# K and V of a batch multiplied a chunk ahead, in front of the next chunk's queries, in a three-stage kernel on one core

## The chip, the cores and the metric

One Trainium2 chip, one of its cores. The metric is the device time of the whole program in microseconds (us), the median over the timed runs. A profiled execution is a run of its own, with its own time beside its span.

## The reference

Three stages in a row. Linear attention (8 batches, 8 heads, 576 tokens, 64 wide), a layer of three maxima and an output product, then routed experts (top 2 of 8):

```python
kv  = einsum('bhsd,bhse->bhde', k, v)            # 64x64 for each batch and head
out = einsum('bhsd,bhde->bhse', q, kv)
x   = out / sqrt(mean(out * out, -1) + 1e-6) * g_norm     # then as (4608, 512)
h   = maximum(maximum(x @ w1, x @ w2), x @ w3)            # 512 -> 768
x   = h @ w_out                                           # 768 -> 512
# top-2 of 8 experts by noisy logits; out[token] += weight * (relu(x @ w1[e]) @ w2[e])
```

## The kernel before

The 4608 tokens go through attention and the first layer in nine chunks (0 to 8) of 512 tokens. A batch has 576 tokens, so chunk c reads the products of K and V (here: K/V) of batches c - 1 and c; they lie in two tiles `kvt`, one for even and one for odd batches.

A chunk c from 1 on has 18 steps g. Each step first runs `misc1(c, g)` and then one first product `g1` (12 matmuls; 512 columns wide, in chunk 1 only 256), which takes the next of a ring of four PSUM banks (`hbank`). VectorE or ScalarE reads the bank afterwards. After the 18 steps comes the window, `window(c)`: the second products `g2` (L399), into the other four banks (`abank`), mixed with the preparation of the next chunk's input. Chunk 0 is the start and is ordered by a planner with costs; the two K/V blocks of batches 0 and 1 are multiplied in it.

`misc1` holds what is put between the steps. At step 0 SP is given the noise, the next chunk's queries (`load_q`, L169) and, in three parts, K and V of the next batch (`load_kv`: a megabyte into `KV0` at L152, a megabyte into a staging tile `STG[b % 2]` at L156, a quarter megabyte into `STG[2]` at L160). At step 7 (chunk 1) or 10 (later) the routing of the chunk before is computed, with two small bf16 products on TensorE (L457, L458) and four scatters on POOL (L472). At step 10 of chunks 1 to 6 the K/V of batch c + 1 is multiplied, `kv_all` (L187) into four banks of the second ring, a bank for two heads, and copied to `kvt` by four copies (L198). At steps 12 to 15 `attend(c + 1, ...)` makes the next chunk's attention: step 12 multiplies the queries (`ao`, L213, four banks of the second ring), squares on ScalarE (L230) and reductions on VectorE (L234) follow, then the normed rows are split in planes (into `KV0`) and turned by DMA transposes on SP (L301). At step 12 (chunk 1) or 14 (later) a copy on VectorE (L480) overwrites a column of the rows that the first scatters read, and four more scatters follow.

A K/V block is 40 matmuls of the program: 32 over 128 rows of K (a tile of 128x64 of the array, two of them side by side), and 8 over the last 64 rows (tiles of 64x64). The trace has two records for each. The queries' block is 64 matmuls of 64x64 tiles. The first and second products use the whole array, 128x128. Every engine works through its instructions in the order of the program; SP gives out its transfers in order too, and one whose buffer is not free yet holds up those behind it.

```python
        for g in range(18):          # chunk c
            misc1(c, g)
            if c > 0:
                g1(c, g)
```

Of the kernel before, what the change touches and what calls it, by code (L numbers as in the profile page):

```python
# [18 lines left out]
NB, NH, S, D = 8, 8, 576, 64  # L19
# [63 lines left out]
def body(tc, A, dbg=None):  # L83
    nc = tc.nc
    PE, ACT, DVE, POOL, SP = nc.tensor, nc.scalar, nc.vector, nc.gpsimd, nc.sync
# [19 lines left out]
    KB = [sb1.tile([128, 256], F, name=f"kvt{i}") for i in range(2)]  # L105
# [15 lines left out]
    def hbank():  # L121
        cnt["h"] += 1
        return HB[(cnt["h"] - 1) % 4]

    def abank():
        cnt["a"] += 1
        return AC[(cnt["a"] - 1) % 4]
# [19 lines left out]
    def quarters(t):  # L147
        return [t[:, i * 512:(i + 1) * 512] for i in range(4)]

    def load_kv(b, part):  # L150
        if part == 0:
            SP.dma_start(KV0, A["kv4"][b, 0])  # L152
            kvraw[b] = [quarters(KV0)]
        elif part == 1:
            t = STG[b % 2]
            SP.dma_start(t, A["kv4"][b, 1])  # L156
            kvraw[b].append(quarters(t))
        else:
            t = STG[2]
            SP.dma_start(t[:, 0:512], A["kvr"][b])  # L160
            kvraw[b].append(t[:, 0:512])
# [3 lines left out]
    def qv(c):  # L165
        return qbuf[c][:, 0:2048].rearrange("p (a t) -> p a t", a=4)
# [8 lines left out]

    HALF = [slice(0, 64), slice(64, 128)]

    def kv_mm(b, p, s, out):
        r = kvraw[b]
        for h in range(2):  # L180
            if s < 4:
                k, v = r[s // 2][2 * (s % 2):2 * (s % 2) + 2]
                o = p * 128 + h * 64
            else:
                k, v = r[2][HALF[p // 2], 0:256], r[2][HALF[p // 2], 256:512]
                o = p % 2 * 128 + h * 64
            PE.matmul(out[HALF[h], :], k[:, o:o + 64], v[:, o:o + 64], start=s == 0, stop=s == 4)  # L187

    def kv_all(b, banks):
        for p in range(4):  # L190
            for s in range(4):
                kv_mm(b, p, s, banks[p][:, 0:64])
        for p in (0, 2, 1, 3):
            kv_mm(b, p, 4, banks[p][:, 0:64])

    def kv_outs(b, banks):
        for p in range(4):
            (ACT.copy if p % 2 else DVE.tensor_copy)(KB[b % 2][:, p * 64:(p + 1) * 64], banks[p][:, 0:64])  # L198
# [3 lines left out]
    def ao(c, j, banks):  # L202
        for h in range(2):
            ao_bank[c, 2 * j + h] = banks[h]
        for i in range(2):
            t0 = (2 * j + i) * 128
            for p in range(4):
                o = slice(i * 256 + p * 64, i * 256 + (p + 1) * 64)
                for x in range(2):
                    t = t0 + x * 64  # L210
                    kb = KB[(c * CT + t) // S % 2]
                    for h in range(2):
                        PE.matmul(banks[h][HALF[x], o], qv(c)[HALF[h], p, t:t + 64],  # L213
                                  kb[HALF[h], p * 64:(p + 1) * 64], start=True, stop=True)
# [6 lines left out]
    def norm_a(c, i, x=None):  # L221
        if x is None:
            x = XNS[xn_n[0] % 4]
            xn_n[0] += 1
        norm_sq(c, i, x)
        norm_red(c, i)
# [9 lines left out]
    def norm_b1(c, i0, i1):  # L236
        s = [ST[:, r, i0:i1, :] for r in range(2)]
        DVE.tensor_scalar(s[0], s[0], 1.0 / 64, 1e-6, op0=OP.mult, op1=OP.add)
        ACT.activation(s[1], s[0], AF.Ln)
        ACT.activation(s[1], s[1], AF.Exp, scale=-0.5)  # L240

    def norm_b2(c, i0, i1):
        s = [ST[:, r, i0:i1, :] for r in range(4)]
        DVE.tensor_tensor(s[2], s[1], s[1], op=OP.mult)
        DVE.scalar_tensor_tensor(s[2], s[2], -0.5, s[0], op0=OP.mult, op1=OP.mult)
        DVE.scalar_tensor_tensor(s[3], s[2], 1.5, s[1], op0=OP.add, op1=OP.mult)

    def norm_c(c, i):
        x = xn_of[c, i]
        DVE.tensor_tensor(x.rearrange("p (h e) -> p h e", h=8),  # L250
                          ao_bank[c, i].rearrange("p (h e) -> p h e", h=8),
                          ST[:, 3, i, :].unsqueeze(2).to_broadcast([128, 8, 64]), op=OP.mult)
# [51 lines left out]
    def planes_in(c, b):  # L304
# [8 lines left out]
        ACT.activation(hi, m, AF.Copy, scale=gn[:, 0:1])  # L313
        DVE.scalar_tensor_tensor(lo, m, gn[:, 0:1], hi.bitcast(F), op0=OP.mult, op1=OP.subtract)

    def attend(c, n):
        if n == 0:
            for j in range(2):
                ao(c, j, [abank(), abank()])
        if n < 2:  # L320
            for b in (2 * n, 2 * n + 1):
                norm_a(c, b)
        if n == 1:
            norm_b1(c, 0, 4)
            norm_b2(c, 0, 4)
        if n in (2, 3):
            j = n - 2
            for b in (2 * j, 2 * j + 1):
                norm_c(c, b)
                planes_out(c, b)  # L330
            planes_turn(c, j)
# [589 lines left out]
    def misc1(c, g):  # L921
        if c == 1 and g == 0:
            fills()
        if c == 1 and (g == 0 or 8 < g < 14):
            f = max(g - 8, 0)
            hsplit(f, early(f), 0, 256)
        if g == 0:
            SP.dma_start(noise[c % 2], A["noise"][c])
        if g == 0 and 0 < c < NCH - 1:
            load_q(c + 1)  # L930
            if c + 1 < NB:
                for i in range(3):
                    load_kv(c + 1, i)
        if c > 0:
            if g == 1:
                ra[c] = route_a(c - 1)
            if 0 < g < 5:
                next(ra[c], None)
            if g == (7 if c == 1 else 10):
                route_b(c - 1)  # L940
                scatter(c - 1, 0)
                if c > 1:
                    zero_out(c - 2)
            if g == (12 if c == 1 else 14):
                scatter(c - 1, 1)
        if 0 < c < NB - 1 and g == 10:
            banks = [abank() for p in range(4)]
            kv_all(c + 1, banks)
            kv_outs(c + 1, banks)
        if 0 < c < NCH - 1 and g >= 12:  # L950
            attend(c + 1, g - 12)
        if c == NCH - 1:
            if g == 11:
                spec_pick()
                load_regs(0, spi[0:1, 0:1], spi[0:1, 1:2])
                regE[1] = regE[0]
                regS[1] = SP.value_load(spi[0:1, 2:3], min_val=0, max_val=DUMMY)
                for p in range(2):
                    load_pair(p)
            if g == 12:  # L960
                load_rows(0)
            if g > 14:
                splits(1)
# [41 lines left out]
    c = NCH - 1  # L1005
# [11 lines left out]
    n, g, q, r2, r1, a = (s8[:, k] for k in (0, 1, 2, 3, 4, 10))  # L1017
# [432 lines left out]
```

## Time and profile before

| | us |
|---|---|
| median of 3 runs | 1510.59 |
| lowest and highest | 1510.12, 1511.88 |
| the profiled execution's own time | 1503.61 |
| its span in the trace | 1501.8 |
| granted TensorE clock in it | 0.998 |

How to read it: the span runs from the first to the last profiled instruction; the profiled execution's own time also has what lies around it. Times in the rows are counted from the start of the span. PE is TensorE's matmuls, PEld its weight loads, DVE VectorE, ACT ScalarE, POOL GpSimd, SP the engine that gives out most transfers. Matmuls overlap, so what a block takes is read from start to start, not from the durations.

### The profile page before, as it was taken

How to read it: one execution, taken by the hardware profiler on the slowest of the kernel's cores; microseconds unless marked ns; L12 is line 12 of the kernel's file. 1: busy time of each engine (PE TensorE's matmuls, PEld its weight loads, DVE VectorE, ACT ScalarE, POOL GpSimd, SP SyncE). 2: the span in 40 equal slices, each digit the busy share in tenths (PEclk: the TensorE clock that was granted, in tenths of full speed). 3: DMA queues.
4: the chain of work that ended last, by engine and by line, in shares of the span. 5: the costliest groups of instructions: out<-in, count | busy, mean ns of one | idle time of the engine just before them, and what ended most of it. 6: DMA issues, size and time to landing. Idle time of an engine off the chain costs nothing.

```text
span 1501.8 us, 22899 instructions
## 1 busy us (share of the span) xinstructions
PE 1476.2 (98%) x9190; PEld 1260.4 (84%) x9190; DVE 749.5 (50%) x1513; ACT 644.2 (43%) x1020; POOL 223.3 (15%) x332
## 2 busy tenths in 40 slices
PE   6999999999999999999999999999999999999997
PEld 6889989898989888888888878887888888888886
DVE  6985545454444444458344454553454374444443
ACT  4653524242424233334444454544454364444443
POOL 0000111102020202023211102202211111110112
PEclk9999999999999999999999999999999999999999
DMA  7412435142332303083776668767565587554555
GB/s 315 144 70 99 152 117 149 72 149 86 126 114 99 121 29 122 0 240 107 200 200 140 173 217 227 194 186 199 135 162 137 147 216 196 132 135 140 139 121 108
DMA packets 160724, 218.43 MB, mean 145 GB/s; under 512 B 124320, under 2 KB 124704, under 8 KB 145120
## 3 DMA queue, kind: packets, MB, share of 16 engines
q1 hardware_dynamic: 140624, 165.14, 35.0%
q0 software_dynamic: 19984, 51.73, 15.1%
q8 instruction: 74, 1.21, 0.3%
q14 instruction: 42, 0.34, 0.1%
HBM read 137.86 MB, written 51.72 MB: 126 GB/s over the span
## 4 chain that ended last, share of the span: by engine, by line
PE 54%; POOL 0%; issue 0%; ACT 0%; POOLq 0%
PE bank L1242 26%; PE bank L1180 26%; PE bank L1194 1%; PE bank L1283 1%; PE bank L1298 0%; PE bank L399 0%; POOL out L1216 0%; PE bank L1205 0%; ACT W L334 0%; PE bank L1289 0%; ACT xn L1247 0%; POOLq L1398 0%; ACT RA L406 0%; PE bank L1136 0%; POOL spacer L1215 0%
## 5 line engine op out<-in xcount | busy, mean ns | idle before, releaser
L353 PE MATMUL bank<-B,W 128*128 128x512 f32 (+1 forms) x2184 | 453.1, 367 | 2.2 <-ACT W L532 2.1
L353 PEld LDWEIGHTS bank<-B,W 128*128 128x128 f32 x2184 | 376.4, 188 | 70.4 <-ACT W L532 2.5
L1242 PE MATMUL bank<-W,B 128*128 128x512 f32 x1704 | 411.2, 390 | 0.0
L1242 PEld LDWEIGHTS bank<-W,B 128*128 128x128 f32 x1704 | 318.6, 188 | 64.5
L1180 PE MATMUL bank<-B,W 128*128 128x512 f32 (+4 forms) x1536 | 361.0, 374 | 0.0
L1180 PEld LDWEIGHTS bank<-B,W 128*128 128x128 f32 x1536 | 278.1, 188 | 53.7 <-issue 4.4
L335 DVE TENSOR_TENSOR W<-G,W 128x1024 fp32r<-128x1024 f32 x168 | 203.0, 1224 | 121.8 <-ACT W L334 121.3
L1184 ACT ACTIVATE B<-bank 128x512 fp32r<-128x512 f32 (+4 forms) x152 | 85.8, 565 | 334.3 <-PE bank L1180 334.3
L1185 DVE SCALAR_TENSOR_TENSOR B<-bank,B 128x512 fp32r<-128x512 f32 (+4 forms) x152 | 98.7, 649 | 249.0 <-ACT B L1184 248.4
L334 ACT ACTIVATE W<-G 128x1024 fp32r<-128x1024 f32 x168 | 175.4, 1055 | 43.5 <-PE bank L1242 24.9
L399 PE MATMUL bank<-W,B 128*128 128x256 f32 (+1 forms) x1296 | 161.0, 284 | 0.4 <-DVE B L361 0.2
L399 PEld LDWEIGHTS bank<-W,B 128*128 128x128 f32 x1296 | 159.5, 188 | 1.6 <-ACT RA L406 0.5
L472 POOL DMA_INDIRECT Xg<-RA,si x72 | 70.7, 981 | 582.0 <-issue 403.7
L371 DVE TENSOR_TENSOR hm<-hm,bank 128x512 f32<-128x512 f32 (+1 forms) x107 | 69.6, 651 | 115.2 <-PE bank L353 109.8
L1216 POOL DMA_INDIRECT out<-xn,idt x36 | 59.2, 1644 | 402.9 <-ACT xn L1247 397.6
L357 ACT ACTIVATE B<-hm 128x512 fp32r<-128x512 f32 (+1 forms) x53 | 32.2, 607 | 172.4 <-DVE hm L371 172.4
L1180 PE MATMUL bank<-xlo,W 128*128 128x512 f32 (+2 forms) x288 | 73.3, 376 | 0.0
L1180 PEld LDWEIGHTS bank<-xlo,W 128*128 128x128 f32 x288 | 52.5, 188 | 9.8
L369 ACT ACTIVATE hm<-bank 128x512 f32<-128x512 f32 (+1 forms) x54 | 30.4, 564 | 64.1 <-PE bank L353 52.2
L406 ACT COPY RA<-bank 128x256 uint16<-128x256 uint16 x72 | 25.6, 372 | 68.6 <-DVE RA L406 63.2
L1216 POOL DMA_INDIRECT out<-hm,idt x20 | 31.9, 1593 | 131.2 <-ACT hm L1247 127.4
L361 DVE TENSOR_TENSOR B<-hm,B 128x512 fp32r<-128x512 f32 (+1 forms) x53 | 35.1, 661 | 32.2 <-ACT B L357 32.2
(230 smaller groups left out, 1034.8 us busy)
## 6 DMA issues: line engine op xcount, KB each, us to landing
G<-mw SPq DMA_DIRECT2D x84, 1024.0 KB, 5.1
G<-w1s SPq DMA_DIRECT2D x12, 1024.0 KB, 4.9
kv<-kv SPq DMA_DIRECT2D x8, 1024.0 KB, 7.1
G<-kv SPq DMA_DIRECT2D x8, 1024.0 KB, 9.2
RB<-qT SPq DMA_DIRECT2D x8, 1024.0 KB, 4.9
G<-mw SPq DMA_DIRECT2D x16, 512.0 KB, 6.4
out<-pad POOLq DMA_DIRECT2D x5, 1280.0 KB, 6.5
out<-pad POOLq DMA_DIRECT2D x2, 1536.0 KB, 6.7
```

Source lines behind the costliest of these rows:

```text
L334: ACT.activation(w[:, 0:1024], src, AF.Copy)
L335: DVE.tensor_tensor(w[:, 1024:2048], src, w[:, 0:1024].bitcast(F), op=OP.subtract)
L353: PE.matmul(bank[:, 0:t1 - t0], w_in(g)[:, a, k, s], x[b][:, k, t0:t1], start=n == 0 and k == 0, stop=n == 2 and k == 3)
L361: DVE.tensor_tensor(h[:, 1], hm, h[:, 0].bitcast(F), op=OP.subtract)
L371: DVE.tensor_tensor(hm, hm, bank, op=OP.max)
L399: PE.matmul(x2b[i][z][:, 0:hi - lo], h[:, a, s], w[:, b, lo:hi], start=f == 0 and n == 0, stop=f == 5 and n == 2)
L472: i = POOL.indirect_dma_start(out=Xg, out_offset=bass.IndirectOffsetOnAxis(ap=idx, axis=0), in_=src, in_offset=None)
L1180: PE.matmul(bank[:, 0:n], w[:, a, k, s], x[b][:, k, 0:n], start=z == 0, stop=z == 11)
L1184: ACT.activation(h[:, 0, 0:n], bank[:, 0:n], AF.Relu)
L1185: DVE.scalar_tensor_tensor(h[:, 1, 0:n], bank[:, 0:n], 0.0, h[:, 0, 0:n].bitcast(F), op0=OP.max, op1=OP.subtract)
L1216: d = POOL.indirect_dma_start(out=A["out"], out_offset=bass.IndirectOffsetOnAxis(ap=idt[u % 3][:, i:i + 1], axis=0), in_=y, in_offset=None ...
L1242: PE.matmul(obank[i], h[:, a, s], w[:, b, ff % 2, :], start=ff == 0 and n == 0, stop=ff == 7 and n == 2)
```

## The change

K/V of a batch is multiplied one chunk earlier than before: at step 12 of chunk c the block of batch c + 2 runs, directly before the products of the queries of chunk c + 1, which use the K/V of batches c and c + 1. Batch 2 is multiplied in chunk 1 at step 5, and batch 3 is loaded right after it; after that K and V of batch c + 2 are loaded at step 0 of chunk c. The block takes two banks of the ring of the first products, two pairs of heads to a bank side by side (the `start` and `stop` marks are set once for a bank), and is copied to `kvt` by two copies, behind the queries' products in the program.

```diff
-    def kv_mm(b, p, s, out):
+    def kv_mm(b, p, s, out, two=False):
...
-            PE.matmul(out[HALF[h], :], k[:, o:o + 64], v[:, o:o + 64], start=s == 0, stop=s == 4)
+            PE.matmul(out[HALF[h], :], k[:, o:o + 64], v[:, o:o + 64], 
+                      start=s == 0 and not (two and p % 2), stop=s == 4 and not (two and p % 2 == 0))
...
+    def kv_next(b, c=None):
+        two = [hbank() for i in range(2)]
+        banks = [two[p // 2][:, p % 2 * 64:p % 2 * 64 + 64] for p in range(4)]
+        kv_all(b, banks, True)
+        if c is not None:
+            ao_all(c)
+        for i in range(2):
+            (ACT.copy if i else DVE.tensor_copy)(KB[b % 2][:, i * 128:i * 128 + 128], two[i][:, 0:128])
+
+    def ao_all(c):
+        for j in range(2):
+            ao(c, j, [abank(), abank()])
+
     def attend(c, n):
         if n == 0:
-            for j in range(2):
-                ao(c, j, [abank(), abank()])
+            if c + 1 < NB:
+                kv_next(c + 1, c)
+            else:
+                ao_all(c)
...
             load_q(c + 1)
-            if c + 1 < NB:
-                for i in range(3):
-                    load_kv(c + 1, i)
+            for i in range(3):
+                if c == 1:
+                    load_kv(2, i)
+                elif c + 2 < NB:
+                    load_kv(c + 2, i)
...
-        if 0 < c < NB - 1 and g == 10:
-            banks = [abank() for p in range(4)]
-            kv_all(c + 1, banks)
-            kv_outs(c + 1, banks)
+        if c == 1 and g == 5:
+            kv_next(2)
+            for i in range(3):
+                load_kv(3, i)
```

## Rows read from the trace of the kernel before

**Rows 1.** The page, part 1: busy time, share of the span, instructions.

```profile
PE 1476.2 (98%) x9190; PEld 1260.4 (84%) x9190; DVE 749.5 (50%) x1513; ACT 644.2 (43%) x1020; POOL 223.3 (15%) x332
```

**Rows 2.** Waits of TensorE, 34 to 720 us: us in total, times, longest.

```profile
PE bank L353 <- ACT W L532: 2.1, 1, 2.1
...
```

**Rows 3.** Windows: each engine's busy us (instructions), PEclk, DMA share, GB/s.

```profile
182.00:720.00 538.00, 537.84 (x3904) 466.20 (x3903) 256.91 (x772) 183.98 (x335) 84.47 (x152) 1.00 0.34 113
```

**Rows 4.** Time line of TensorE, chunk 2: start us, us, what.

```profile
209.55 0.19 PE L457 MATMUL bank<-Cb,onesb 128*128 128x40 bf16 x1
...
209.98 0.40 PE L187 MATMUL bank<-G 128*64 128x64 f32 x8
...
211.38 0.79 PE L187 MATMUL bank<-G 128*64 128x64 f32 x24
212.10 5.73 PE L353 MATMUL bank<-B,W 128*128 128x512 f32 x24
...
236.25 1.01 PE L399 MATMUL bank<-W,B 128*128 128x256 f32 x7
```

**Rows 5.** Time line of TensorE, chunk 7.

```profile
566.92 0.19 PE L457 MATMUL bank<-Cb,onesb 128*128 128x40 bf16 x1
...
591.12 1.14 PE L399 MATMUL bank<-W,B 128*128 128x256 f32 x8
```

**Rows 6.** Time line of TensorE, chunk 8.

```profile
635.90 0.19 PE L457 MATMUL bank<-Cb,onesb 128*128 128x40 bf16 x1
...
657.81 1.38 PE L399 MATMUL bank<-W,B 128*128 128x256 f32 x10
```

**Rows 7.** Time line of TensorE, chunk 2, a window of 0.5 us.

```profile
211.71 0.46 PE L187 MATMUL bank<-G 64*64 64x64 f32 x16
```

**Rows 8.** Time line of SP's queue at the start of chunk 1.

```profile
131.96 0.33 SPq L169 DMA_DIRECT2D RB<-qT  x1
132.34 0.43 SPq L152 DMA_DIRECT2D kv<-kv  x1
132.81 0.42 SPq L156 DMA_DIRECT2D G<-kv  x1
```

**Rows 9.** DMA issues, 120 to 170 us (us to landing); L156, all six loads.

```profile
RB<-qT SPq DMA_DIRECT2D x1, 1024.0 KB, 4.8
kv<-kv SPq DMA_DIRECT2D x1, 1024.0 KB, 6.9
G<-kv SPq DMA_DIRECT2D x1, 1024.0 KB, 8.9
...
Xg<-RA,si POOLq DMA_INDIRECT x8, 2.8
...
DMA to landing us min/median/max: 8.9/9.3/10.4
```

**Rows 10.** Time line of TensorE, chunk 1.

```profile
133.93 10.22 PE L353 MATMUL bank<-B,W 128*128 128x256 f32 x84
144.00 0.19 PE L457 MATMUL bank<-Cb,onesb 128*128 128x40 bf16 x1
...
148.53 0.45 PE L187 MATMUL bank<-kv 128*64 128x64 f32 x8
148.82 0.40 PE L187 MATMUL bank<-G 128*64 128x64 f32 x8
...
150.22 0.79 PE L187 MATMUL bank<-G 128*64 128x64 f32 x24
...
154.00 2.10 PE L213 MATMUL bank<-kvt,RB 64*64 64x64 f32 x128
```

**Rows 11.** Time lines of POOL and VectorE, chunk 1, and of VectorE, chunk 2.

```profile
151.33 0.97 POOL L472 DMA_INDIRECT Xg<-RA,si  x1 [0.22 <-ACT kvt L198]
...
155.69 0.17 DVE L480 COPY RA<-wt 128x4 f32<-128x4 f32 x1
...
217.87 0.69 DVE L371 TENSOR_TENSOR hm<-hm,bank 128x512 f32<-128x512 f32 x1 [1.96 <-PE bank L353]
```

More of the change, by code (lines that the diff above doesn't have):

```diff
@@ L186, in kv_mm, with kv_all @@
                 o = p % 2 * 128 + h * 64
-            PE.matmul(out[HALF[h], :], k[:, o:o + 64], v[:, o:o + 64], start=s == 0, stop=s == 4)
-    def kv_all(b, banks):
+            PE.matmul(out[HALF[h], :], k[:, o:o + 64], v[:, o:o + 64],
+                      start=s == 0 and not (two and p % 2), stop=s == 4 and not (two and p % 2 == 0))
+    def kv_all(b, banks, two=False):
         for p in range(4):
             for s in range(4):
-                kv_mm(b, p, s, banks[p][:, 0:64])
+                kv_mm(b, p, s, banks[p][:, 0:64], two)
         for p in (0, 2, 1, 3):
-            kv_mm(b, p, 4, banks[p][:, 0:64])
+            kv_mm(b, p, 4, banks[p][:, 0:64], two)
     def kv_outs(b, banks):
```

## The prediction

> **What bounds the kernel now.** I read the page first, then who TensorE waited for, then the stretch in which the diff acts. The page says that TensorE is busy for 98% of the span [rows 1]. A share alone would not settle it, because the stages differ, so the second view is the list of TensorE's waits from 34 us, when the start is over, to 720 us, when the chunks are done: its largest entry is a single wait of 2.1 us [rows 2]. From 182 to 720 us TensorE is busy for 537.84 of 538 us, at a granted clock of 1.00, while VectorE and ScalarE are busy for less than half of it [rows 3]. So in the chunks the order on TensorE is the time: what an edit adds to or takes from TensorE's own sequence moves the end one for one, and what it does to VectorE, ScalarE or the queues costs nothing until TensorE waits for it. Each term below is therefore a stretch of TensorE's time line, and each risk is a new wait on TensorE.
>
> 0.2% is 3.0 us, about what a measurement of this kernel can tell from no change.
>
> **What the K/V block costs where it stands.** In chunk 2 the block sits behind the routing product of step 10, and the queries' block (L213) follows two steps later. From the routing product to the first product of the window it is 236.25 - 209.55 = 26.70 us [rows 4]. Chunk 7 has the same stretch without K/V: 591.12 - 566.92 = 24.20 us [rows 5]. Chunk 8 has neither K/V nor queries: 657.81 - 635.90 = 21.91 us [rows 6]. So a K/V block on its own costs 26.70 - 24.20 = 2.50 us of TensorE, and the queries' block 24.20 - 21.91 = 2.29 us.
>
> Now how much of the 2.50 us is edges, that is, time at the change from one kind of product to another. In the middle of the block eight records take (211.38 - 209.98) / 6 = 0.233 us [rows 4]. The 64 records over full K rows are eight such groups, 1.87 us. The last 16 records, of tiles of 64x64, run four at a time, four groups at the pace of the pairs (0.058 us), 0.23 us. Together 2.10 us, so 0.40 us are edges. One of them lies inside the block, where the tiles change from 128x64 to 64x64: from 211.38 to 211.71 is 0.33 us for eight records, 0.10 us above the pace [rows 4, 7]. It can reach 0.15 us if the first 64x64 products are slow too: 211.71 to 212.10 is 0.39 us for 0.23 us of work, and that 0.16 us need not all be the block's exit. So the outer edges (into the block, and out into 128x128 again) are 0.25 to 0.30 us.
>
> **The change part by part.**
>
> K/V in front of the queries. For batches 3 to 7, in chunks 1 to 5, the block ends with 64x64 tiles, and the queries' block is of 64x64 tiles from its first product. I take it that the meeting costs nothing, because no shape changes there. Then the inner edge stays, the queries' block pays its own edges as it does now, and the outer edges of K/V are gone: 0.25 us a chunk, 5 x 0.25 = 1.25 us saved. Bounds: nothing, if the meeting costs as much as an outer edge; 0.40 us a chunk, 2.0 us, if even the inner one went.
>
> A rule of the Trainium skill bears on this: TensorEngine Tiling (Array Packing), Key Properties, says that a change of tiling mode, unlike a change of tile within a mode, drains the array. It gives no price. By it a chunk now has five changes for both blocks and would have three, so two of them go. The edges of both blocks are 0.40 + 2.29 - 1.87 = 0.82 us by the rows above (32 groups of four at 0.058 us for the queries), so 0.16 us for each of five, 0.33 us a chunk and 1.6 us in all. The trace agrees on the sign, with edges wherever the shape changes; I keep the 1.25 us of my sum, since the inner edge shows a smaller price than the mean.
>
> The one block that stays alone. Batch 2 is multiplied in chunk 1 at step 5 in place of step 10, between first products as now: the same 2.50 us, no difference. Chunk 6 has no K/V block any more. Six blocks before, six after.
>
> Copies. Four of 128x64 become two of 128x128, queued behind the queries' products in the program, so before the squares on ScalarE. The next chunk is the first to read them. VectorE and ScalarE have half their time free [rows 3], so nothing.
>
> The first load in chunk 1. Its issue does not move: SP gives out the queries at 131.96 us, batch 2's first half at 132.34 and its second half at 132.81 [rows 8], landing 6.9 and 8.9 us later, at 139.24 and 141.71 us [rows 9]. What moves is the need. Seven steps of chunk 1 take 144.00 - 133.93 = 10.07 us, 1.44 each, so step 5 begins at 141.12 us; the second half is wanted 148.82 - 148.53 = 0.29 us into the block, with its entry about 141.45 us [rows 10]. So it is late by about 0.25 us, and TensorE waits for it with everything behind it. The rest, a quarter of the size, goes out right behind and is used 150.22 + 0.23 - 148.53 = 1.9 us into the block, some 1.6 us after the second half: in time. Bounds: nothing; or, with the longest landing of the six such loads, 10.4 us, at 143.2 us, a wait of 1.75 us [rows 9].
>
> The second load in chunk 1 is new in place: batch 3 is asked for at step 5, into the buffers that batch 2 is being multiplied from. Its first half waits on SP for the last product that reads that buffer, which is over before the last row of the block, 150.22 - 148.53 = 1.7 us into it [rows 10]: 141.20 + 1.7 + 0.25, about 143.15 us. Nothing stands behind it on SP before the transposes of step 14. In the train of [rows 8] the first megabyte landed 4.8 us after its issue and the second 139.24 - 131.96 = 7.3 us after the first's issue; so the halves would be there at 148.0 and 150.4 us, and the rest before the 143.15 + 9.75 = 152.9 us at which a third whole megabyte would be (141.71 - 131.96 = 9.75). The queries of step 12, which K/V now precedes, start at 154.00 us today with one K/V block before them, and would again have one before them: 154.25 us with the wait. More than 3 us to spare; with the longest landing, 10.4 us, still 154.0 us. Cost nothing; if the cover went, each us of lateness is a us.
>
> What else is late in chunk 1. Step 7's routing moves by 2.75 us, so the fourth scatter that starts at 151.33 on POOL would start at 154.1 and land 2.8 us later, at 156.9 us. VectorE's copy L480 of step 12 overwrites a column that those scatters read; it ran at 155.69 and would stand until 156.9 us [rows 9, 11]. Behind it on VectorE are the copy of a K/V bank, the reductions and the maximum of step 13. The reductions need the queries' products, which follow K/V from 154.25 on, 2.25 us for the one and 1.87 for the other, about 158.4 us; the maximum comes more than a step later still. Hidden. In later chunks the loads go out at step 0 for step 12 instead of step 10: more time than now.
>
> The ring. K/V takes two of the first products' four banks, so steps 12 to 15 of a chunk use a bank two places on. The two that it takes were read long before (the routing's and step 9's). Step 13 needs step 11's bank, which VectorE reads for 0.69 us as soon as its products end (from 217.87 us in chunk 2) [rows 11]; until step 13 begins TensorE has 2.25 us of K/V, 2 us of queries and step 12 to do. No wait.
>
> **Sum.** 1503.61 us for the profiled execution; -1.25 + 0.25 = -1.0 gives 1502.6. The median of the runs is 6.98 us above that execution; I carry the difference over: 1510.59 - 1.0 = 1509.6 us. That is -0.07%, within what counts as the same.
>
> **Rivals.** (a) The meeting is an edge like the others: nothing saved, the 0.25 us wait stays, 1510.8 us. For it: every change of line in the trace that I can price costs something. Against: the price goes with the shape, and here it does not change. (b) The first load is later than in this profile: 1.75 - 1.25 = +0.5, 1511.1 us. For it, the spread of the landing rows; against, this very load took 8.9 us here. (c) Slower: the ring is short by the two banks, and in each of five chunks a first product waits for a reading of a bank, 0.69 us as the rows price it [rows 11]: 3.45 + 0.25 - 1.25 = +2.45, 1513.0 us; it counts as slower from (3.0 + 1.0) / 5 = 0.8 us a chunk. Against it: the readings named above are over in time. (d) Batch 3 lands late at step 12; that decides from 154.25 + 4.0, about 158.3 us, 15 us after its issue, where 10.4 is the longest in sight.
>
> **How the numbers follow.** Forecast 62 in 100, (a) 17, (b) 11, (c) 4, (d) 2; 4 are left for a gain beyond the edges that I can price. Range: the runs before lay from 0.5 us below to 1.3 us above their median. The larger saving without a wait gives 1508.6, less 0.5 is 1508.1; (b) plus 1.3 gives 1512.4. I give 1508.0 to 1512.3. Faster by over 0.2%: the 4, and 4 for a forecast of 1 us read as 3. Slower by over 0.2%: half of (c), (d), and 3 for (b) read as more. Same: 85.
>
> **What would show it.** Right: chunks 2 to 5 from routing to window about 26.45 us in place of 26.70, chunk 6 24.2; TensorE goes from L187 to L213 without a gap; one wait of some tenths for a load near 141.4 us in chunk 1; no other new wait on TensorE. Wrong: an edge of 0.2 us or more at the meeting, a wait near 154 us, or waits of the first products for a bank.

## The result, and the profile after

The changed kernel takes 1518.62 us (median of 6 runs, 1516.94 to 1524.42), the kernel before 1510.19 us beside it (6 runs, 1508.3 to 1511.88): a ratio of 1.0062, 95% interval 1.0051 to 1.0074. It is slower by 0.6%, and the prediction, 1509.6 us in a range up to 1512.3, was wrong. The profiled execution took 1516.94 us, its span 1515.1 us, at a granted TensorE clock of 0.995.

TensorE still looks busy, now with 5.5 us more than in [rows 1], from the page's first part:

```profile
PE 1481.7 (98%) x9190; PEld 1263.3 (83%) x9190; DVE 750.2 (50%) x1507; ACT 644.1 (43%) x1014; POOL 222.8 (15%) x332
```

The waits of TensorE from 34 to 720 us (columns as in [rows 2]) tell more. Before, the one wait of 2.1 us for `W` led a list with nothing else above a few tenths. Now there are 12 more, 7.8 us in total, and nothing that the profile shows ended them. The profile calls such a wait "issue".

```profile
PE bank L369 <- issue: 3.5, 3, 2.7
PE bank L214 <- issue: 2.6, 5, 1.0
PE bank L369 <- ACT W L548: 2.1, 1, 2.1
PE bank L187 <- issue: 1.7, 4, 0.4
...
PE bank L187 <- DMA G<-kv: 0.2, 1, 0.2
```

Lines have moved: the first products are L369 (L353 before), the second L415 (L399), the queries' products L214 (L213), the scatters L488 (L472); K/V is L187 as before. The time line of TensorE shows where the waits stand: the block of batch 2 in chunk 1, the step behind the two blocks in chunk 2, the two blocks in chunk 3.

```profile
143.04 0.45 PE L187 MATMUL bank<-kv 128*64 128x64 f32 x8
143.66 0.45 PE L187 MATMUL bank<-G 128*64 128x64 f32 x8 [0.17 <-DMA G<-kv]
...
227.96 2.11 PE L369 MATMUL bank<-B,W 128*128 128x512 f32 x8
232.77 9.52 PE L369 MATMUL bank<-B,W 128*128 128x512 f32 x34 [2.71 <-issue]
...
299.38 0.45 PE L187 MATMUL bank<-kv 128*64 128x64 f32 x8
...
300.60 0.28 PE L187 MATMUL bank<-G 128*64 128x64 f32 x3
301.29 0.36 PE L187 MATMUL bank<-G 128*64 128x64 f32 x5 [0.42 <-issue]
301.46 0.42 PE L187 MATMUL bank<-kv 128*64 128x64 f32 x8
301.70 0.81 PE L187 MATMUL bank<-G 128*64 128x64 f32 x24
302.33 2.05 PE L214 MATMUL bank<-kvt,RB 64*64 64x64 f32 x128
304.31 1.89 PE L369 MATMUL bank<-B,W 128*128 128x512 f32 x7
```

The first load in chunk 1 is waited for as forecast, 0.17 us. K/V goes over into the queries' products at 302.33 without a gap. In the middle of K/V, though, eight records take 0.23 us up to 300.60, and then nothing starts until 301.29. POOL's time line says what lies there: the routing's scatters (L488) and the zero filling of the output (L621), until 301.38.

```profile
295.71 0.96 POOL L488 DMA_INDIRECT Xg<-RA,si  x1 [51.28 <-issue]
...
299.53 0.97 POOL L488 DMA_INDIRECT Xg<-RA,si  x1 [0.21 <-issue]
300.49 0.89 POOL L621 DMA_DIRECT2D out<-pad  x1
```

The windows over chunk 2 (columns as in [rows 3]) show the long wait and what follows: in 226 to 230 us the DMA engines are full, from 230 on TensorE is idle, and when it starts again its granted clock is 0.61, the mean of its two levels with 1.2 GHz for most of the stretch.

```profile
226.00:230.00 4.00, 4.00 (x148) 3.50 (x141) 1.57 (x3) 1.26 (x3) 0.89 (x2) 1.00 1.01 371
230.00:232.80 2.80, 0.10 (x2) 0.03 (x1) 0.00 (x0) 0.00 (x0) 0.00 (x0) 1.00 0.93 351
232.80:237.00 4.20, 4.20 (x12) 3.29 (x12) 1.46 (x3) 2.02 (x5) 0.00 (x0) 0.61 0.04 13
```

### The profile page after: what moved, and what is told of

The parts are those of the page before. It is cut to its first block, busy times and chain, and to the rows that moved or that the text cites. A ratio compares the mean times of both kernels' runs of the same rounds, so it can differ in the third digit from the quotient of the medians.

```text
span 1515.1 us, 22889 instructions
## 1 busy us (share of the span) xinstructions
PE 1481.7 (98%) x9190; PEld 1263.3 (83%) x9190; DVE 750.2 (50%) x1507; ACT 644.1 (43%) x1014; POOL 222.8 (15%) x332
## 3 DMA queue, kind: packets, MB, share of 16 engines
q8 instruction: 74, 1.21, 0.3%
## 4 chain that ended last, share of the span: by engine, by line
PE 96%; DMA 1%; DVE 1%; issue 1%; ACT 1%; POOL 0%; SPq 0%; POOLq 0%; DVEq 0%
PE bank L369 29%; PE bank L1260 26%; PE bank L1198 26%; PE bank L415 10%; PE bank L187 1%; PE bank L214 1%; DMA G<-kv 1%; PE bank L1212 1%; PE bank L1301 0%; PE bank L1316 0%; DVE stat L235 0%; PE bank L273 0%; POOL out L1234 0%; PE bank L559 0%; ACT W L548 0%
## 5 line engine op out<-in xcount | busy, mean ns | idle before, releaser
L369 PE MATMUL bank<-B,W 128*128 128x512 f32 (+1 forms) x2184 | 456.0, 369 | 5.7 <-issue 3.5
L369 PEld LDWEIGHTS bank<-B,W 128*128 128x128 f32 x2184 | 378.3, 189 | 75.0 <-issue 5.6
L415 PE MATMUL bank<-W,B 128*128 128x256 f32 (+1 forms) x1296 | 160.5, 284 | 0.2 <-DVE B L377 0.2
L415 PEld LDWEIGHTS bank<-W,B 128*128 128x128 f32 x1296 | 159.3, 188 | 1.1 <-DVE B L377 0.5
L488 POOL DMA_INDIRECT Xg<-RA,si x72 | 70.4, 978 | 596.8 <-issue 408.9
```

The costliest lines, as they stand in the source:

```text
L369: PE.matmul(bank[:, 0:t1 - t0], w_in(g)[:, a, k, s], x[b][:, k, t0:t1], start=n == 0 and k == 0, stop=n == 2 and k == 3)
L415: PE.matmul(x2b[i][z][:, 0:hi - lo], h[:, a, s], w[:, b, lo:hi], start=f == 0 and n == 0, stop=f == 5 and n == 2)
L488: i = POOL.indirect_dma_start(out=Xg, out_offset=bass.IndirectOffsetOnAxis(ap=idx, axis=0), in_=src, in_offset=None)
```

## The experiments

Theory S, formed first: TensorE is not given its instructions as fast as the small products use them up, and two blocks in a row are dense for twice as long. Rival R: the place itself costs it, by the two ring banks, the copies or the meeting of the blocks. The runs fell on five chips, each used on one occasion. The kernel before stood beside them with medians of 1510.29 us (e1 to e4), 1509.53 (e5 to e8), 1510.41 (e9 to e12), 1505.96 (e13 to e16) and 1510.36 (e17, e18). Each ratio is against the kernel before on the same chip.

**e1_again**: the kernel before, nothing changed, for a second profile.

> The kernel before, unchanged. Both theories: ratio 1.000, within 0.2%. What it is for: whether its profile again has no wait of TensorE put down to issue in the chunks (theory S, the instructions of TensorE come too late where small products stand close together, expects none or one short one, since 80 and 128 matmul records stand apart), and whether the half clock that the changed kernel showed at 42 us in chunk 0 comes here too (then about 1.8 us of the difference between the two profiles is not of the change).

1510.35 us, ratio 0.9999 [0.999, 1.0008]. Its profile (own time 1510.12, span 1508.3 us) is not that of [rows 10]: the same K/V block, in the same place 1.3 us behind the first scatter, now stalls. The time line of TensorE in chunk 1, with POOL's first scatter:

```profile
148.71 1.14 POOL L472 DMA_INDIRECT Xg<-RA,si  x1 [109.64 <-DVE hm L371]
150.04 0.45 PE L187 MATMUL bank<-kv 128*64 128x64 f32 x8
...
152.26 0.22 PE L187 MATMUL bank<-G 128*64 128x64 f32 x1 [0.41 <-issue]
...
153.02 0.33 PE L187 MATMUL bank<-kv 128*64 128x64 f32 x3 [0.37 <-issue]
153.75 0.22 PE L187 MATMUL bank<-kv 128*64 128x64 f32 x1 [0.40 <-issue]
...
154.50 1.14 PE L187 MATMUL bank<-G 128*64 128x64 f32 x20 [0.39 <-issue]
155.56 3.69 PE L353 MATMUL bank<-B,W 128*128 128x256 f32 x21
```

Eight records in 0.233 us became a few matmuls every 0.74 us. A wait of 1.02 us stands in the queries' block of chunk 7 as well:

```profile
580.07 1.52 PE L213 MATMUL bank<-kvt,RB 64*64 64x64 f32 x85 [1.02 <-issue]
```

So the kernel before can have such waits too, and this execution, which has them, takes as long as the timed runs; the one that was profiled for the prediction had none. The expectation's second question has its answer as well: the half clock in chunk 0 comes here too (granted clock 0.70 from 40 to 44 us, 1.00 in the first profile), and chunk 1 begins 1.5 us later (135.44 against 133.93 us). The changed kernel's profile, whose chunk 1 begins at 135.76 us, owes 1.8 us to this and not to the change (in e17, the same kernel again, it begins at 133.69).

**e2_apart**: K/V a chunk ahead in the two ring banks, but at step 10 (chunk 1: 11), apart from the queries.

```diff
-    KB = [sb1.tile([128, 256], F, name=f"kvt{i}") for i in range(2)]
+    KB = [sb1.tile([128, 256], F, name=f"kvt{i}") for i in range(3)]
...
-            if c + 1 < NB:
-                kv_next(c + 1, c)
-            else:
-                ao_all(c)
+            ao_all(c)
...
+        if 0 < c < NB - 2 and g == (11 if c == 1 else 10):
+            kv_next(c + 2)
```

> The changed kernel with a third tile for K/V, so that the same block, a chunk ahead, in the same two banks of the same ring and with the same loads, can run at step 10 (step 11 in chunk 1), one or two first products ahead of the queries. Theory S: the waits put down to issue in the blocks of chunks 2 to 5 and the 2.7 us one go, the two blocks cost 2.5 and 2.3 us again, and the time is 1510 to 1513 us (ratio 1.000 to 1.002). Rival R (the ring that is short by two banks, or the loads moved a chunk ahead): nothing that it blames is changed, so 1517 to 1520 us (ratio 1.005 to 1.007).

1509.61 us, 0.9998 [0.9989, 1.0007]. No wait in chunks 2 to 5; 0.45 us in chunk 1, 1.06 us in each of 6 and 7. The banks, the copies and the earlier loads cost nothing: R is left with the meeting.

**e3_twice**: the kernel before with each K/V block made twice in its place.

```diff
-            kv_all(c + 1, banks)
+            for _ in range(2):
+                kv_all(c + 1, banks)
```

> The kernel before with the matmuls of K/V made twice over at step 10, the second time over the first; ring, loads and queries as before. 320 instructions stand together in place of 160. Six blocks at 2.1 us of work more: 12.6 us, 1523 us (ratio 1.0083) if nothing else happens, which is what rival R expects, without any wait put down to issue. Theory S: on top of that such waits in the block or behind it in most of the six chunks, 0.4 us and more each, 1526 to 1536 us (ratio 1.010 to 1.017).

1554.79 us, 1.0292 [1.0276, 1.0308]. The added work is 6 x 2.1 = 12.6 us at the pace of [rows 4]; the time is 44.5 us more. That is far more than either theory expected. TensorE stalls in the second half of each block, which runs on when POOL has begun, with no queries beside it: the meeting isn't needed.

**e4_pad**: 32 small products at the start, so that all later instructions lie elsewhere in the blocks in which they are loaded.

```diff
+    for _ in range(32):
+        PE.matmul(HB[3][:, 0:16], ones, ones[:, 0:16], start=True, stop=True)
```

> The kernel before with 32 small bf16 products (64 instructions, results unused) added at the start, where TensorE waits for VectorE anyhow: at most 1.5 us of work, most of it hidden. It shifts every later instruction of TensorE by a quarter of a 16 KB block of the instruction fetch. Theory S: where the blocks of K/V and of queries fall in the fetched blocks matters, so waits put down to issue may come or go in single chunks: a change of -2 to +6 us that the work does not explain. Rival R: 0 to +1.5 us, no such wait.

1511.01 us, 1.0004 [0.9995, 1.0013]; the waits stand where they stood in e1_again.

**e5_one_step**: e2_apart with K/V at step 11 in all chunks.

```diff
-        if 0 < c < NB - 2 and g == (11 if c == 1 else 10):
+        if 0 < c < NB - 2 and g == 11:
```

> The kernel of e2_apart with the block at step 11 in every chunk: one first product (24 instructions in 2.7 us) between K/V and queries in place of two. Theory S (TensorE's instructions arrive in blocks of 16 KB and 416 small ones in 4.2 us outrun them): one first product is time enough for one more block, so 1509 to 1512 us (ratio 0.999 to 1.001) and at most two short waits in chunks 2 to 5. If any nearness is bad, 1512 to 1516 us.

1523.73 us, 1.0091 [1.0075, 1.0106], where e2_apart, one step earlier, loses nothing. Neither theory expected that much. Each K/V block of chunks 2 to 5, alone, has three or four waits. In chunk 3 they end at 296.30, 297.02, 297.75 and 298.45 us, while POOL is at the scatters and the zero filling from 292.87 to 298.54. Its last scatter and TensorE's last wait there:

```profile
296.69 0.96 POOL L485 DMA_INDIRECT Xg<-RA,si  x1 [0.22 <-issue]
298.45 0.88 PE L187 MATMUL bank<-G 128*64 128x64 f32 x17 [0.49 <-issue]
```

Density alone, S, does not tell step 10 from step 11; where POOL stands does.

**e6_halves** and **e7_full**: the changed kernel, first with each block split between steps 12 and 13, then with K/V on the whole array (20 larger matmuls, some 10.5 us more work in all).

```diff
+    def kv_half(b, j):
+        t = kv_bank[b, j] = hbank()
+        for s in range(5):
+            for k in range(2):
+                kv_mm(b, 2 * j + k, s, t[:, k * 64:k * 64 + 64], k)
...
-        if n == 0:
+        if n < 2:
             if c + 1 < NB:
-                kv_next(c + 1, c)
-            else:
-                ao_all(c)
+                kv_half(c + 1, n)
+            ao(c, n, [abank(), abank()])
...
```

```diff
+            if two:
+                if h == 0:
+                    PE.matmul(out, k[:, o:o + 128], v[:, o:o + 128], start=s == 0 and p % 2 == 0, stop=s == 4 and p % 2 == 1)
+                continue
...
```

> The changed kernel with each block cut in two: half of K/V and half of the queries at step 12, the other halves at step 13; ring, loads and the chunk ahead as in the change. About 208 instructions stand together in place of 416. Theory S: the waits put down to issue go from chunks 2 to 5 and from the queries of chunks 6 and 7; the second pair of edges costs what the first saved (about 0.4 us a chunk), so 1508 to 1512 us (ratio 0.9985 to 1.001). Rival A (what costs is that the two blocks meet, their shapes or their banks, not how many instructions stand together): they meet twice as often, so 1518 us or more.

> The changed kernel with K/V on the whole array, both heads of a pair in one matmul (half of each result is not used): 20 matmuls in place of 40, so 336 instructions in 5.9 us in place of 416 in 4.2, in the same place. TensorE works some 1.75 us longer on each of six blocks, 10.5 us. Theory S: the waits put down to issue shrink in chunks 1 to 5, and the time is 1518 to 1522 us, about that of the change with 10 us more work. Rival A: the blocks meet as before, so the change's time and the work, 1527 to 1531 us.

Halves: 1520.72 us, 1.0071 [1.0058, 1.0085]; the waits of chunks 3 to 5 are smaller (0.29 us), those of chunks 6 and 7 as long as before (0.99 and 1.03), and chunk 1 has five, 1.7 us. Full: 1526.75 us, 1.011 [1.0095, 1.0125]; no wait in chunks 3 to 5, where four such matmuls take 0.45 us, but 2.1 us in chunk 1, 3.48 in chunk 2 and 1.0 in each of 6 and 7. Both times miss what S expected and are nearer to rival A's, that the meeting costs it. The waits speak against A: in chunks 3 to 5 they shrink or go although the blocks still meet, and e3 and e5 have them without a meeting.

**e8_mix**: e2_apart with the queries of chunks 6 and 7 split between two steps.

```diff
-            ao_all(c)
+            if c < 7:
+                ao_all(c)
+        if c >= 7 and n < 2:
+            ao(c, n, [abank(), abank()])
```

> The kernel of e2_apart with the queries' block in two halves, steps 12 and 13, in chunks 6 and 7 alone, where e2_apart showed a wait of 1.06 us in each. Theory S: 128 in place of 256 instructions together, the two waits go (-2.1 us), a pair of edges comes in each (+0.8 us): about 1.3 us below e2_apart, ratio to the kernel before 0.998 to 1.000. If the waits of those chunks have another cause, they stay and it is 0.8 us slower than e2_apart.

1510.85 us, 1.0003 [0.9994, 1.0012], and a wait of 1.0 us still in each of chunks 6 and 7. The expectation missed: half a block stalls as a whole one does. Theory S falls here. Theory S2 takes its place: **a block of small products stalls where it lies under POOL's giving out of scatters**, about 5.7 us from 2 us behind the routing's products. In chunk 7 of e1_again the wait ends at 580.07 us, POOL's last issue at 580.17; in chunk 3 of the changed kernel 301.29 and 301.38 (above). That last issue is the zero filling; the scatters' part ends 0.8 us before the waits do, and e12 tells the two apart. Before, K/V at step 10 takes those first 2 us, and pushes the queries of step 12 just behind POOL's end.

**e9_spread**: the changed kernel with the scatters moved away from the blocks, together with the routing's products and the zero filling, which stand in the same step.

```diff
-            if g == (7 if c == 1 else 10):
+            if g == (7 if c == 1 else 6):
                 route_b(c - 1)
                 scatter(c - 1, 0)
...
-            if g == (12 if c == 1 else 14):
+            if g == (15 if c == 1 else 14):
                 scatter(c - 1, 1)
```

> The changed kernel, K/V where the change puts it, but GpSimd's four scatters, which had stood two steps ahead of the block, go out at step 6 (in chunk 1 at step 7 as now, where the other four move from step 12 to step 15), so that no block of small products lies under them. Theory S2 (TensorE is short of instructions only where a dense block of small products lies under GpSimd's scatters): the waits of 0.4 to 1.0 us that nothing releases go from the K/V and queries' blocks of chunks 1 to 7, and the half clock behind them; the edges saved stay; some 10 to 14 us less than the changed kernel, 1504 to 1508 us, below both kernels. Theory S (the small products outrun the supply of instructions by their density alone): the waits stay where they are and so does the time, about 1518 us.

1504.99 us, 0.9966 [0.9952, 0.9979]: faster than both kernels. From 50 us on no wait is put down to "issue". The two blocks took 304.31 - 299.38 = 4.93 us in chunk 3 of the changed kernel. Here they take 4.28 us, as the time line of chunk 2 shows:

```profile
220.16 0.45 PE L187 MATMUL bank<-kv 128*64 128x64 f32 x8
...
221.84 0.79 PE L187 MATMUL bank<-G 128*64 128x64 f32 x24
222.46 2.05 PE L214 MATMUL bank<-kvt,RB 64*64 64x64 f32 x128
224.44 7.80 PE L369 MATMUL bank<-B,W 128*128 128x512 f32 x33
```

**e10_early**: the same for the kernel before (in chunk 1 its K/V block moves a step as well). **e11_onto**: the opposite, its routing and scatters pushed onto K/V.

```diff
-            if g == (7 if c == 1 else 10):
+            if g == (5 if c == 1 else 6):
...
-            if g == (12 if c == 1 else 14):
+            if g == 14:
...
-        if 0 < c < NB - 1 and g == 10:
+        if 0 < c < NB - 1 and g == (11 if c == 1 else 10):
```

```diff
-            if g == (7 if c == 1 else 10):
+            if g == (7 if c == 1 else 9):
```

> The kernel before, K/V at step 10 as it was, with the routing and the first four scatters at step 6 (chunk 1: step 5), the other four at step 14 in all chunks, and chunk 1's K/V block at step 11. Theory S2: the waits in the K/V block of chunk 1 (about 1.6 us and the half clock behind them) and in the queries' block of chunk 7 (1.0 us and the half clock) go: 1504 to 1508 us. Theory S: K/V and queries are as dense as before, nothing changes: about 1510 us.

> The kernel before with the routing and the scatters one step earlier, at step 9, so that GpSimd's scatters of chunks 2 to 6 lie on the K/V block of step 10; K/V itself isn't touched. Theory S2: each of these five blocks is now short of instructions and loses some 3 to 4.5 us with the half clock behind it, chunk 7's wait in the queries' block goes: 1522 to 1532 us. Theory S, and any theory in which the two blocks side by side or the banks are the cause: about 1510 us.

Early: 1506.52 us, 0.9978 [0.9968, 0.9988], no wait put down to "issue"; a new one of 1.4 us, as chunk 1's routing now comes before VectorE has what it multiplies ready. Onto: 1518.14 us, 1.0048 [1.0032, 1.0063]. The sign is S2's, the size half of the expected: POOL begins 0.98 us into the block (217.34 against 216.36 us), so only its last part stalls, and a chunk takes 72.9 us in place of 71.47, 7.1 us in five (chunks 2 to 6). The time line of chunk 2:

```profile
217.34 0.97 POOL L472 DMA_INDIRECT Xg<-RA,si  x1 [49.75 <-ACT hm L369]
219.34 0.36 PE L187 MATMUL bank<-G 64*64 64x64 f32 x6 [0.36 <-issue]
```

**e12_no_zero**: the changed kernel with the zero filling put off to step 16.

```diff
-                if c > 1:
-                    zero_out(c - 2)
+            if g == 16 and c > 1:
+                zero_out(c - 2)
```

> The changed kernel with the zero filling of the scattered rows' other buffer moved from the scatters' step to step 16; the scatters stay. Theory S2 with full DMA queues behind chunk 2's long wait: that wait of 2.7 us in the second block of chunk 2 and the half clock behind it go, about 1514 us, while the waits of 0.3 to 1.0 us of chunks 1 and 3 to 7 stay. If the scatters alone make the long wait: it stays, about 1518 us.

1521.41 us, 1.0071 [1.0054, 1.0088], so the total missed. The wait of 2.7 us in chunk 2 is gone as expected, and 0.32 to 0.46 us remain in each of chunks 2 to 5, 1.0 us in each of 6 and 7. Chunks 1 to 7 take 482.7 us, 4.2 less than in the changed kernel's first profile. Two other waits are new, from the list of TensorE's waits:

```profile
PE bank L415 <- ACT RA L422: 5.6, 1, 5.6
...
PE bank L369 <- DVE hm L387: 1.3, 1, 1.3
```

The longer one stands in the window of chunk 8, behind ScalarE, which had waited for a load; that the moved filling held up this load is likely, but not shown. The other stands in chunk 1, ahead of the first moved filling, and is not its work. So the long wait of chunk 2 needed the filling. It needed more than that: in e1_again the DMA engines are as full behind the same filling (share 1.01 from 226 to 230 us) and no wait follows. The short waits need only the scatters. In both kernels the last of them in a chunk ends 0.7 to 0.9 us behind the end of the last scatter, with a filling behind it (in chunk 3 of the changed kernel 300.50 and 301.29 us) and without one, as here in chunk 3 (294.15 and 294.85):

```profile
293.18 0.97 POOL L488 DMA_INDIRECT Xg<-RA,si  x1 [0.21 <-issue]
294.85 0.41 PE L187 MATMUL bank<-kv 128*64 128x64 f32 x7 [0.32 <-issue]
```

**e13 to e18**: what about the scatters does it? The spread kernel, e9_spread, with something put under the blocks again at step 11: twelve fillings of a tile on POOL (e13), a megabyte sent by SP (e14), four scatters more (e15), four plain transfers by POOL (e16).

```diff
+    def under(c):
+        DVE.memset(trig, 0.0)
+        POOL.tensor_copy(junk, trig)
+        for i in range(4):
+            POOL.memset(spacer, 0.0)
+            at = bass.IndirectOffsetOnAxis(ap=si[(c - 1) % 2][:, i:i + 1], axis=0)
+            d = POOL.indirect_dma_start(out=dump, out_offset=at, in_=rows[:, i, :].bitcast(U16), in_offset=None)
...
+        if 0 < c < NCH - 1 and g == 11:
+            under(c)
```

(This is e15, and e18 too; e13 has `POOL.memset(pad[:, 0:512], 0.0)` in the loop, e14 one `SP.dma_start` and e16 four `POOL.dma_start` from `pad` to `dump`.)

> The kernel with the scatters spread out (K/V in front of the queries, the first scatters at step 6), and in chunks 1 to 7 twelve fillings of a tile by GpSimd, some 6 us without a transfer, set off at step 11 so that they lie under the blocks of small products. Theory A (GpSimd at work is enough to hold back TensorE's instructions): waits of 0.3 to 1 us in each block, 3 to 6 us a chunk, 1525 to 1545 us. Theories B and C (it takes transfers, or GpSimd giving them out): no new wait, about 1505 us.

> The kernel with the scatters spread out, and in chunks 1 to 7 one plain transfer of a megabyte, given out by SP at step 11, so that its packets fill the DMA queues under the blocks of small products while GpSimd is idle. Theory B (bytes in the queues are what holds back TensorE's instructions): waits in each block, 1515 to 1545 us. Theories A and C: no new wait, about 1505 us.

> The kernel with the scatters spread out, and in chunks 1 to 7 four more scatters of the same rows by GpSimd, into a tensor that nothing reads, set off at step 11 so that they lie under the blocks of small products. Theory C (GpSimd giving out transfers holds back TensorE's instructions): waits of 0.3 to 1 us in the blocks of chunks 1 to 7, some 3 to 6 us a chunk with the half clock behind them, 1525 to 1545 us. If the four scatters do nothing here, the theory of the scatters falls: about 1505 us.

> As the run with four more scatters, but the four transfers that GpSimd gives out are plain ones of the same size, without a list of rows. Theory C as it stands, any transfer that GpSimd gives out (some 0.9 us each in its time line): waits as with four more scatters, 1520 to 1545 us. If only the scatter through a list of rows does it: about 1505 us.

1508.1, 1507.23, 1506.97 and 1504.6 us, ratios 1.0012 [1.0001, 1.0023], 1.0007 [0.9997, 1.0018], 1.0008 [0.9999, 1.0018] and 0.9991 [0.9981, 1.0]. The scatters did not do what S2 expected; but the kernel before was 4 us faster here as well. In e15_four_more, four scatters lie on the blocks of chunk 2 from 216.86 to 221.76 us, and TensorE runs through them at full pace:

```profile
218.24 0.45 PE L187 MATMUL bank<-kv 128*64 128x64 f32 x8
...
219.93 0.79 PE L187 MATMUL bank<-G 128*64 128x64 f32 x24
220.54 2.29 PE L214 MATMUL bank<-kvt,RB 64*64 64x64 f32 x128
222.76 3.51 PE L369 MATMUL bank<-B,W 128*128 128x512 f32 x14
```

Some waits are left there, in the queries' blocks of chunks 3 and 5: 0.2 and 0.4 us with the scatters, 1.4 and 0.9 with SP's megabyte (and 1.6 behind the blocks of chunk 2), 1.1 and 0.7 with POOL's plain transfers, none with POOL's fillings. So transfers that are no scatters can hold TensorE up as well: theory B, the bytes, is not refuted, and here they did more than the scatters.

**e17_after_again**, **e18_four_more**: the changed kernel, and e15's kernel once more, together on another chip.

> The changed kernel once more, unchanged. In the last four runs the kernel before took 1505.96 us on the chip they had, 4 us less than on the other chips, and blocks under GpSimd's transfers ran there without waits. Theory D (the waits under the scatters are a matter of the chip): where the kernel before takes about 1506 us, the changed one has none of the waits that nothing releases and is not slower, 1503 to 1506 us; where the kernel before takes about 1510 us, it has them and takes 1516 to 1521 us. Theory S2 alone (the scatters over a dense block do it on every chip): some 8 us above the kernel before on any chip.

> The kernel with the scatters spread out and four more of them under the blocks, as run before on a chip where the kernel before takes 1505.96 us. Where the kernel before takes about 1510 us, theory C (GpSimd giving out scatters holds back TensorE's instructions) with theory D expects waits of 0.3 to 1 us in the blocks of chunks 1 to 7 and 1515 to 1545 us; where it takes about 1506 us, the same as before, about 1507 us. If it stays near 1507 us on a chip where the kernel before takes 1510 us and the changed kernel has its waits, the scatters alone are not the cause.

The changed kernel: 1517.49 us, 1.0055 [1.0042, 1.0068], with waits in the same chunks as in its first profile (8.8 us in all, 7.8 there). The kernel with four more scatters: 1536.57 us, 1.0177 [1.0162, 1.0192], 29.6 us above the same kernel on the chip before, and 31.6 above e9_spread, which is the same kernel without these scatters (beside it the kernel before took 1510.41 us, here 1510.36). Its chunk 2, TensorE and then POOL:

```profile
226.39 0.45 PE L187 MATMUL bank<-kv 128*64 128x64 f32 x8
...
227.84 0.28 PE L187 MATMUL bank<-kv 128*64 128x64 f32 x2
228.47 0.35 PE L187 MATMUL bank<-kv 128*64 128x64 f32 x5 [0.35 <-issue]
229.22 0.22 PE L187 MATMUL bank<-kv 128*64 128x64 f32 x1 [0.39 <-issue]
...
229.93 0.22 PE L187 MATMUL bank<-G 128*64 128x64 f32 x1 [0.37 <-issue]
230.64 0.96 PE L187 MATMUL bank<-G 128*64 128x64 f32 x21 [0.49 <-issue]
231.37 3.45 PE L214 MATMUL bank<-kvt,RB 64*64 64x64 f32 x128
234.75 3.47 PE L369 MATMUL bank<-B,W 128*128 128x512 f32 x14
```

```profile
225.01 1.06 POOL L947 DMA_INDIRECT dump<-RA,si  x1 [0.17 <-issue]
...
228.95 0.97 POOL L947 DMA_INDIRECT dump<-RA,si  x1 [0.23 <-issue]
```

Both blocks take 234.75 - 226.39 = 8.36 us, against 4.52 in e15_four_more, behind the same scatters at the same distance. Part of it is the clock: the windows (columns as in [rows 3]) show it at 1.00 while TensorE stands, and at 0.57 from 231 us on:

```profile
228.00:231.00 3.00, 1.40 (x22) 0.74 (x17) 0.57 (x1) 0.00 (x0) 1.77 (x4) 1.00 0.63 244
231.00:235.00 4.00, 4.00 (x146) 3.93 (x146) 1.15 (x3) 1.26 (x3) 0.00 (x0) 0.57 0.07 23
```

So C and D hold as far as they go: scatters given out under a dense block stall it on four of the five chips, and hardly on the fifth. As each chip was used on one occasion, the chip and the occasion can't be told apart. That POOL's other work or SP's bytes do not do the same on such a chip isn't shown, as e13, e14 and e16 ran where the scatters themselves hardly did.

## Why the prediction was wrong

Chunk by chunk, from the start of its first products to those of the next, in us, worked out from the time lines of TensorE:

| chunk | before, profiled first | before, e1_again | changed | e9_spread |
|---|---|---|---|---|
| 1 | 48.41 | 52.44 | 54.35 | 50.99 |
| 2 | 71.47 | 71.48 | 76.38 | 71.21 |
| 3, 4, 5 (each) | 71.47 | 71.47 | 71.85 | 71.21 to 71.48 |
| 6 | 71.47 | 71.47 | 70.30 | 68.94 |
| 7 | 68.98 | 70.31 | 70.26 | 68.94 |
| 1 to 7 | 474.75 | 480.12 | 486.85 | 474.05 |

- **The order on TensorE is the time**: right. Between the two kernels' profiles with waits the chunks differ by 486.85 - 480.12 = 6.7 us, the spans by 1515.1 - 1508.3 = 6.8. The medians differ by 8.4 us; the other 1.6 are in neither profile. Executions of the changed kernel differ among themselves (1516.94 to 1524.42 us; e17's profile has 488.9 us for the same chunks).
- **Edges, -1.25 us**: right in kind, nearly in size. The meeting costs nothing, and with the waits gone chunks 2, 3 and 4 take 0.26, 0.19 and 0.26 us less than before, for 0.25 forecast. Chunk 5 shows no gain, nor does chunk 1, which takes 2.58 us more for its second block where chunk 6 takes 2.53 less. Sum 0.7 us. The prediction's estimate by the rule of the Trainium skill, TensorEngine Tiling (Array Packing), Key Properties, that a change of mode drains the array, was 1.6 us; the trace agrees with the rule in kind, and not with that sum.
- **The first load, +0.25 us**: 0.17. The second load, the ring, the copies and the scatter's copy of chunk 1: no wait, as forecast, and e2_apart shows the same for a whole kernel. Rivals (a), (c) and (d) did not occur, and of (b) only the forecast wait.
- **The whole sum, -1.0 us**: on executions without waits it holds: 474.05 - 474.75 = -0.7 us.
- **The step that failed** is in the sum: "The median of the runs is 6.98 us above that execution; I carry the difference over", with all waits but those for a bank or a load put at nothing. The difference was not a constant. In e1_again, whose own time is that of the timed runs, 5.4 us of it are waits and their half clock in two places, chunk 1's K/V (52.44 - 48.41 = 4.0) and chunk 7's queries (70.31 - 68.98 = 1.3), and both lie under POOL's scatters; another 1.5 us lie ahead of chunk 1, with the half clock there. A cost that hangs on what lies under the scatters cannot be carried over when the change moves a block. That the first profile came from a chip like that of e13 to e16 fits its blocks, as the K/V of chunk 1 ran through three scatters at full pace, and its own time, 1503.61 us. That lies in the 1502.77 to 1509.15 of the kernel before there and below all 72 of its timed runs beside the other kernels, the lowest of which is 1507.93. It is argued, not shown.
- **What took its place**: K/V left the 2 us before POOL starts and went under its last issues, and the queries of chunk 6 no longer have a block ahead of them to hold them until POOL ends, as those of chunk 7 had none before either. Against e9_spread, waits and the clock behind them cost 3.4 us in chunk 1, 5.2 in chunk 2, 0.4 to 0.65 in each of 3 to 5, 1.4 in 6 and 1.3 in 7: 12.8 us in all, against 5.4 in e1_again. Taken together, 12.8 - 5.4 - 0.7 = 6.7 us, the difference of the profiles. Taking the scatters away from the blocks, with the routing and the filling (e9, e10), undoes it; moving the filling alone leaves the short waits (e12); and four scatters that nothing reads bring the waits back (e18). That shows the scatters as the cause of the short waits, where they occur. The long wait of chunk 2 comes with the filling (e12).
- **"No other new wait on TensorE"** was the line that would show it wrong, and did; the waits named there, for a bank or a load, were not the ones that came.

Open: whether it is the chip or the occasion that differs, and why; by which way the scatters hold TensorE up, by their bytes or by being given out; whether other work of POOL does so; and what the changed kernel would take on the chip of e13 to e16.

## What to carry to other kernels

When the profiled execution is some us faster than every timed run, find where the others lose it before using the profile: here a second profile of the same kernel showed the waits. Keep blocks of many small matmuls away from the stretch in which GpSimd gives out scatters (in e14 a plain megabyte sent just ahead of them was followed by single waits of 0.9 to 1.6 us), and when such a block is moved, look at what POOL's time line has at the new place; here the scatters' place was worth 13.6 us to the changed kernel (1504.99 against 1518.62), the edit itself less than one. Try a cheap reordering on more than one chip before trusting a null result.

## What was not expected of the hardware

- A block of small fp32 matmuls that runs at eight records in 0.233 us falls, under GpSimd's scatters (0.97 us each), to a few matmuls every 0.7 to 0.75 us (e1_again, e18_four_more). The stall outlasts the last scatter by 0.7 to 0.9 us (0.69 in e1_again's chunk 1, 0.82 in the changed kernel's chunk 2, 0.73 in e18_four_more's chunk 2). First products, twelve in 2.84 us ([rows 4]: 24 from 212.10 us, 5.7 us), lay under the same scatters without such a wait in e1_again.
- The same kernel differs by 29.6 us between two chips, with one occasion on each (e15_four_more 1506.97, e18_four_more 1536.57), the kernel before by 4.4 us (1505.96 and 1510.36).
- After such waits the granted clock reads 0.57 to 0.67 over some 4 us, so that a stall costs more than its idle time: 8.36 - 4.52 = 3.84 us in e18_four_more's chunk 2, of which 1.6 us are idle.
- The wait of 2.71 us in chunk 2 falls in a stretch with full DMA engines (share 1.01 from 226 us, 0.93 from 230 us), and one of the changed kernel's 74 transfers of the queue "instruction" (1.21 MB, some 16 KB each) is among those of 230 to 233 us. The Trainium skill, Runtime: NRT & Kernel Launch, Terms, says that an engine's instruction memory is refilled in 16 KiB blocks; the profile's page agrees in size. That the wait was for this block is argued; e12_no_zero, without the filling, shows that it goes with the full queues, and e1_again, with queues as full and no wait, that they alone do not make it.
